# A two-stage attention and mixture-of-experts kernel with another written order

## The chip, the cores and the metric

The kernel runs on one core of a Trainium2 chip, in one launch. The metric is the device time of an execution in microseconds (us), the median of several runs; lower is better. A core has a matrix engine (TensorE, PE in the profile; its weight loads are shown apart as PEld), three engines that work on the elements of tiles (VectorE = DVE, ScalarE = ACT, GpSimd = POOL), and SyncE (SP), which here does nothing but issue DMAs. The engines run side by side, and each takes its own instructions strictly in the order in which the program lists them. They wait for each other by semaphores.

## The reference

The inputs q, k and v hold 8 batches, 8 heads, 576 positions and 64 numbers a head. The first stage is sparse attention: heads 0 to 3 see the last 32 positions ("local"), heads 4 to 7 see every 32nd position back ("strided"). Its result is x, 576 x 512 for each batch. The second stage is a mixture of four experts, each of which is a causal attention with one head of 64; each position uses the two experts with the largest gate logits.

```
scores = where(masks, q @ k.T / 8, -1e9)        # masks: local for heads 0-3, strided for 4-7
x = softmax(scores) @ v                          # heads side by side: 576 x 512 a batch
logits = x @ w_gate                              # 4 experts, the best two kept, softmax over them
for e in range(4):
    a = softmax(causal((x @ wq[e]) @ (x @ wk[e]).T / 8))
    out += weight[e] * (a @ (x @ wv[e]) @ wo[e]) # weight 0 where e is not one of the two
```

## The kernel before

The first stage handles two heads at a time, a "head pair" (hp 0 and 1 local, 2 and 3 strided), in `stage1`: SP loads q, k and v; q and k are transposed, for the first two batches by PE into PSUM banks with copies out of them (`tp`, `tp_out`, lines 570 to 599 and 335), later by DVE (`tq`, line 522); then the scores on PE (`sl`, `s`, lines 627 and 641), the mask and a softmax in six steps that goes between DVE, GpSimd and ACT (lines 655 to 679), a transpose of the weights (`ptl`, or `pt` and `pt_out`) and the product with v (`xal`, `xa`, lines 735 and 754). x is then split into a rounded high part (`xh`, ACT, line 717) and the rest (`xl`, DVE, line 719), so that three fast matmuls stand for one of full precision.

The second stage handles two experts at a time (ep 0 and 1): the projections of q and k (`pj`, lines 907 and 918; for the first two experts of batch 0, line 918, cut into one operation for each head pair, so that they can begin before x is complete), the values and gate logits (`vp`, line 854; for the last rows of two batches together, line 817), scores (`s2`, `s2_4`, lines 992 and 972), mask and maximum on DVE (line 999), exp on ACT (line 1004), scaling by the softmax sum and the gate on GpSimd (`scale2`, lines 1023 and 1029), a transpose on PE (`t2`, line 1048) with copies out of PSUM (`t2_out`, line 335), the product with the values (`acc`, line 1081), and the output projection (`yp`, line 1110) with its copy (`yp_out`, line 335) and store.

None of this is issued in the order in which it is written. The calls only make a list `OPS` of 2573 operations, each of which knows its engine or the two engines that may do it, its dependencies and its buffers. `schedule()` then walks the list ORDER of operation numbers and emits each. So ORDER fixes the order of each engine's queue (what stands earlier in ORDER goes first on its engine), and also which buffer of a ring an operation gets, since a buffer is taken when its first user is emitted. Operations on different engines still run side by side. SECOND is the set of operations that go to the second of their two engines: a copy out of PSUM (`t2_out`, `tp_out`, `pt_out`, `vp_out`, `yp_out`; helper `either`) goes to ACT, and to DVE if it is in SECOND. FILL gives a number of matmuls of an identity matrix with itself that are emitted just before an operation ("filling matmuls", line 298), into a free PSUM bank, if there is one; their result is not used, and they keep PE busy. Before all of them stand five "warm" matmuls (line 1130).

There are 8 PSUM banks; the rings of SBUF buffers for natural q and k hold three (`nat`; pairs 0 and 1 of batch 0 use a tile of the second stage, `p`). Numbers that are needed below: 1 and 2 load q and k of pair 0 of batch 0, 44 and 45 of pair 1, 87 and 88 of pair 2, 122 and 123 of pair 3; 16 and 17 load v of pair 0; 157 to 178 load weights of q and k; 13, 8 and 3 are the transposes of pair 0; 18 its scores, 33 its product with v; 1129 to 1150 are the cut projections of batch 0, 1168 and 1171 the first of its uncut ones, which read x of all four pairs.

Of the kernel before, what the change touches and what calls it, by code (L numbers as in the profile page):

```python
# [20 lines left out]
def attention_moe_kernel(  # L21
# [61 lines left out]
    class Ring:  # L83
# [36 lines left out]
    }  # L120
    ORDER = [
# [1072 lines left out]
```

## Time and profile before

| what | value |
|---|---|
| median of 3 runs (lowest, highest) | 453.73 us (452.95, 453.95) |
| span of the profiled execution, first to last instruction | 452.2 us; its own time beyond the span is not recorded, the median is 1.5 us longer |
| PE busy | 439.5 us, 97% |
| DVE busy | 356.5 us, 79% |
| ACT busy | 264.9 us, 59% |
| GpSimd busy | 221.5 us, 49% |
| granted TensorE clock, mean | 0.995 |
| HBM read and written | 31.20 MB and 9.44 MB |

The profile is one execution. "Busy" is the time in which an engine has at least one instruction under way, and matmuls overlap in a pipeline: a projection's matmul is shown as 0.29 us long, but the next one starts 0.13 us later. What an operation costs PE is therefore read from its start to the start of the next one. [...] A matmul of full precision, such as a filling one, is shown as two instructions.

### The profile page before, as it was taken

The page shows a single profiled execution, that of the slowest core. Times are in us where ns is not written, and L with a number is a line of the kernel's source. Part 1 is how long each engine was busy: PE and PEld are TensorE (multiplying, and loading weights), DVE is VectorE, ACT ScalarE, POOL GpSimd, SP SyncE. Part 2 cuts the span into 40 slices and gives each one's busy share as a digit, 9 for nine tenths or more (in the row PEclk, how much of TensorE's full clock was granted, in tenths as well). Part 3 has the DMA queues.
Part 4 walks back from the last instruction along what each step waited for, and adds up shares of the span by engine and source line. Part 5 has one row for each costly group of instructions (what it writes and reads, how often), then busy time and mean ns, then how long its engine had stood idle before and what let it go on. Part 6 is the DMA issues. An engine that isn't in the chain of part 4 may idle for free.

```text
span 452.2 us, 19227 instructions
## 1 busy us (share of the span) xinstructions
PE 439.5 (97%) x7792; PEld 392.4 (87%) x7792; DVE 356.5 (79%) x1121; ACT 264.9 (59%) x835; POOL 221.5 (49%) x404
## 2 busy tenths in 40 slices
PE   6998999999999999999999999999999999999996
PEld 5887898897899998998899998988988998998875
DVE  4668889989999787769999778789998877466852
ACT  1447647765748455466666566376585477554751
POOL 4163843794563825165647454237743736326330
PEclk9899999999999999999999999999999999999999
DMA  5775465635744524552624525506733201010013
GB/s 146 156 185 159 106 125 120 102 79 83 141 84 89 127 53 101 95 124 57 126 68 93 116 58 117 99 16 127 125 98 89 94 30 53 1 25 25 25 71 116
DMA packets 156272, 41.89 MB, mean 93 GB/s; under 512 B 145976, under 2 KB 149432, under 8 KB 156184
## 3 DMA queue, kind: packets, MB, share of 16 engines
q1 hardware_dynamic: 156184, 40.67, 41.2%
q8 instruction: 61, 1.00, 0.9%
q14 instruction: 27, 0.22, 0.2%
HBM read 31.20 MB, written 9.44 MB: 90 GB/s over the span
## 4 chain that ended last, share of the span: by engine, by line
PE 83%; DVE 9%; ACT 2%; DMA 2%; issue 1%; POOL 1%; SPq 0%; DVEq 0%; ACTq 0%; POOLq 0%
PE bank L907 20%; PE bank L1081 10%; PE bank L854 9%; PE bank L1110 9%; PE bank L992 7%; PE bank L1048 6%; PE bank L735 3%; PE bank L972 3%; PE bank L627 3%; PE bank L754 3%; PE bank L298 3%; PE bank L641 2%; DVE qkt L522 2%; PE bank L705 2%; DVE p L999 1%
## 5 line engine op out<-in xcount | busy, mean ns | idle before, releaser
L1029 POOL TENSOR_SCALAR p<-p,st,wt 128x128 f32<-128x128 f32 (+3 forms) x128 | 77.0, 614 | 51.0 <-DVE st L1013 34.7
L1004 ACT ACTIVATE p<-p,st 128x256 f32<-128x256 f32 (+3 forms) x128 | 71.2, 560 | 8.2 <-DVE st L999 8.2
L999 DVE CUSTOM_DVE_ANT_0 p<-bank,m_cau 128x384 f32<-128x384 f32 (+3 forms) x128 | 57.5, 485 | 4.8 <-PE bank L992 4.1
L1081 PE MATMUL bank<-th,vs 128*64 128x192 f32 (+4 forms) x512 | 48.3, 337 | 0.2 <-DVE th L335 0.2
L522 DVE STREAM_TRANSPOSE qkt<-nat 128x576 f32<-128x576 f32 x48 | 47.4, 1006 | 0.0
L927 ACT CAST qk<-bank 128x288 fp32r<-128x288 f32 x64 | 25.0, 402 | 37.7 <-PE bank L907 34.9
L1081 PEld LDWEIGHTS bank<-th,vs 128*64 128x64 f32 x512 | 34.0, 137 | 13.2 <-issue 6.6
L335 ACT COPY th<-bank 128x256 f32<-128x256 f32 (+2 forms) x105 | 41.3, 433 | 7.1 <-PE bank L1048 6.0
L717 ACT CAST xh<-bank 128x128 fp32r<-128x128 f32 (+4 forms) x112 | 30.0, 321 | 22.6 <-PE bank L754 11.6
L719 DVE TENSOR_TENSOR xl<-bank,xh 128x128 fp32r<-128x128 f32 (+4 forms) x112 | 32.3, 326 | 12.2 <-ACT xh L717 11.8
L1048 PE MATMUL bank<-ident,p 64*128 64x64 f32 x800 | 38.6, 228 | 1.0 <-DVE p1s L655 0.6
L1048 PEld LDWEIGHTS bank<-ident,p 64*128 64x128 f32 x800 | 32.2, 139 | 6.5 <-issue 1.4
L668 POOL TENSOR_TENSOR p1s<-p1s,st 128x648 f32<-128x648 f32 (+1 forms) x18 | 20.8, 1160 | 33.1 <-DVE st L666 30.9
L854 PE MATMUL bank<-wh_v,xh 128*128 128x260 f32 x128 | 36.3, 284 | 0.0
L854 PE MATMUL bank<-wh_v,xl 128*128 128x260 f32 x128 | 36.2, 283 | 0.0
L854 PE MATMUL bank<-wl_v,xh 128*128 128x260 f32 x128 | 36.1, 282 | 0.0
L907 PE MATMUL bank<-xh,wh_q 128*128 128x288 f32 x120 | 36.0, 300 | 0.0
L907 PE MATMUL bank<-xh,wh_k 128*128 128x288 f32 x120 | 35.6, 297 | 0.0
L907 PE MATMUL bank<-xl,wh_q 128*128 128x288 f32 x120 | 35.4, 295 | 0.0
L907 PE MATMUL bank<-xl,wh_k 128*128 128x288 f32 x120 | 35.4, 295 | 0.0
L907 PE MATMUL bank<-xh,wl_q 128*128 128x288 f32 x120 | 35.3, 294 | 0.0
L907 PE MATMUL bank<-xh,wl_k 128*128 128x288 f32 x120 | 35.3, 294 | 0.0
(182 smaller groups left out, 1286.0 us busy)
## 6 DMA issues: line engine op xcount, KB each, us to landing
out_dram<-ys SPq DMA_DIRECT2D x32, 256.0 KB
nat<-in_k_dram SPq DMA_DIRECT2D x96, 72.0 KB
nat<-in_q_dram SPq DMA_DIRECT2D x96, 72.0 KB
v<-in_v_dram SPq DMA_DIRECT2D x96, 40.0 KB
v<-in_v_dram SPq DMA_DIRECT2D x48, 54.0 KB
v<-in_v_dram SPq DMA_DIRECT2D x32, 48.0 KB
v<-in_v_dram SPq DMA_DIRECT2D x32, 45.0 KB
out_dram<-ys SPq DMA_DIRECT2D x8, 128.0 KB
```

What stands on the lines that cost most here:

```text
L335: (nc.scalar.copy if e == "ACT" else nc.vector.tensor_copy)(dst, src)
L522: op("tq", {"DVE": 0.66 if local else 1.11}, k0 - 13, lambda e, x=x: nc.vector.transpose(turned(qkt.t, x), raw(x) if local else raw(x).rea ...
L719: op("xl", {"DVE": dve(n_)}, key + 0.5, lambda e, s_=s_, x_=x_: nc.vector.tensor_sub(x_(xl.t), s_(xa.t), x_(f(xh.t))), r=[xa, xh[u]], w=[x ...
L854: nc.tensor.matmul(vp.t[:, :NV], xx.t[:, t0:t0 + 128], ww.t[:, kt, :], start=i == 0, stop=i == 11)
L907: nc.tensor.matmul(pj.t[:, :HS], ww.t[:, kt, ep * 128:(ep + 1) * 128], xx.t[:, c], start=i == 0, stop=i == 11)
L992: nc.tensor.matmul(sp[a].t[:, :nk], x.t[r, 0, q0:q0 + 128], y.t[r, 1, :nk], start=i == 0, stop=i == 2)
L999: lambda e, sp=sp, p=p, a=a, nk=nk, ci=ci: nc.vector.tensor_tensor_reduce(out=p.t[:, a, :nk], in0=sp[a].t[:, :nk], in1=m_cau[:, S - nk:], ...
L1004: op("exp2", {"ACT": 0.285 + 0.00084 * nk}, k_ + 1, lambda e, p=p, a=a, ci=ci, nk=nk: nc.scalar.activation(p.t[:, a, :nk], p.t[:, a, :nk], ...
L1029: lambda e, p=p, a=a, ci=ci, t=t, nk=nk: nc.gpsimd.tensor_scalar(p.t[:, a, :nk], p.t[:, a, :nk], st.t[:, 20 + ci + a:21 + ci + a], wt.t[:, ...
L1048: nc.tensor.transpose(tp[hf].t[:, 64 * c:64 * c + 64], src, ident[r, r])
L1081: nc.tensor.matmul(acc.t[o, c0:c0 + cn], vw, th[a].t[:, s0:s0 + cn], start=j == 0, stop=j == idx[-1], skip_group_check=True)
L1110: nc.tensor.matmul(yp.t[:, :DM], xx.t[:, c0:c0 + 128], ww.t[:, ep, :], start=i == 0, stop=i == 5)
```

## The change

The three tables are replaced; the operations, their code, their buffers and the rings stay the same. By engine the lists say:

| operations that may go to two engines | before | after |
|---|---|---|
| `t2_out` | 105 ACT, 55 DVE | 119 ACT, 41 DVE |
| `tp_out` | 35 ACT, 21 DVE | 40 ACT, 16 DVE |
| `pt_out` | 23 ACT, 9 DVE | 27 ACT, 5 DVE |
| `yp_out` | 21 ACT, 15 DVE | 23 ACT, 13 DVE |
| `vp_out` | 20 ACT, 12 DVE | 17 ACT, 15 DVE |
| `xf` | 38 ACT, 26 GpSimd | 32 ACT, 32 GpSimd |
| `tq_out` | 4 ACT, 8 GpSimd | 6 ACT, 6 GpSimd |
| filling matmuls in FILL | 77 at 33 places | 26 at 11 places |
| of them with a free bank | 67 | 22 |

The cut diff shows the head of ORDER and FILL whole. The rest of ORDER is permuted in the same way.

```diff
     ORDER = [
-        87, 2, 1, 0, 13, 8, 16, 10, 3, 11, 14, 15, 45, 9, 12, 7, 4, 6, 5, 18, 19, 21, 44, 46, 49, 88, 23, 20, 47, 22,
-        172, 173, 166, 48, 59, 123, 25, 51, 17, 52, 56, 58, 169, 122, 201, 181, 54, 55, 57, 92, 53, 27, 50, 61, 24, 26,
-        28, 29, 31, 93, 60, 89, 91, 30, 62, 64, 90, 66, 94, 63, 96, 32, 65, 68, 33, 67, 127, 70, 69, 97, 71, 98, 99, 72,
-        129, 202, 128, 124, 100, 239, 36, 38, 40, 73, 41, 170, 74, 126, 75, 39, 125, 102, 76, 83, 77, 37, 78, 157, 213,
-        104, 101, 240, 84, 215, 208, 203, 106, 34, 103, 35, 160, 171, 209, 214, 131, 158, 205, 183, 105, 159, 204, 107,
-        174, 1135, 132, 212, 206, 161, 207, 175, 79, 210, 241, 133, 278, 134, 211, 81, 135, 246, 137, 277, 182, 250,
...
+        2, 0, 1, 13, 44, 8, 12, 45, 15, 14, 3, 10, 56, 6, 46, 87, 7, 11, 57, 88, 9, 5, 4, 51, 58, 53, 55, 18,
+        48, 20, 22, 50, 89, 47, 19, 16, 52, 54, 24, 49, 122, 123, 21, 17, 90, 92, 26, 28, 23, 25, 91, 94, 27,
+        202, 29, 31, 93, 201, 59, 239, 61, 63, 62, 64, 96, 30, 124, 65, 32, 66, 68, 127, 97, 126, 67, 128, 99,
+        98, 101, 100, 125, 240, 33, 129, 169, 131, 70, 69, 203, 60, 102, 38, 71, 104, 40, 72, 172, 36, 103, 207,
+        132, 133, 105, 157, 208, 74, 134, 34, 204, 37, 213, 39, 35, 278, 210, 41, 214, 209, 205, 206, 215, 212,
+        277, 73, 75, 135, 170, 308, 241, 244, 246, 247, 76, 106, 250, 173, 81, 211, 79, 80, 136, 251, 83, 77,
+        85, 171, 307, 248, 95, 245, 160, 158, 78, 218, 138, 107, 163, 174, 137, 84, 1147, 242, 82, 130, 219,
...
     ]
     FILL = {
-        13: 6, 3: 3, 18: 5, 51: 4, 92: 8, 89: 1, 96: 1, 33: 4, 127: 1, 124: 7, 76: 3, 1135: 6, 218: 1, 1136: 1, 282: 1,
-        110: 1, 1148: 2, 316: 1, 1131: 4, 1143: 4, 295: 1, 1388: 1, 1206: 1, 1298: 1, 1237: 1, 1408: 1, 1564: 1, 1473:
-        1, 1712: 1, 2070: 1, 2242: 1, 2547: 1, 2550: 1,
+        0: 4, 3: 1, 8: 3, 13: 1, 18: 3, 56: 1, 96: 1, 124: 2, 241: 4, 246: 2, 1137: 4,
     }
```

## Rows read from the trace of the kernel before

**Rows 1.** The page, busy time of each engine (us, share of the span, instructions):
```profile
PE 439.5 (97%) x7792; PEld 392.4 (87%) x7792; DVE 356.5 (79%) x1121; ACT 264.9 (59%) x835; POOL 221.5 (49%) x404
```

**Rows 2.** The page, shares of the chain that ended last, by engine:
```profile
PE 83%; DVE 9%; ACT 2%; DMA 2%; issue 1%; POOL 1%; SPq 0%; DVEq 0%; ACTq 0%; POOLq 0%
```

**Rows 3.** Busy time by stretch (us), then clock, DMA share and GB/s:
```profile
10.30:56.30 46.00, 43.19 (x1067) 38.55 (x1068) 34.05 (x87) 26.31 (x74) 21.27 (x28) 0.96 0.63 153
60.00:150.00 90.00, 88.53 (x1874) 78.89 (x1873) 82.24 (x250) 60.59 (x191) 49.16 (x85) 1.00 0.56 106
100.00:140.00 40.00, 39.98 (x915) 33.40 (x919) 38.04 (x116) 24.85 (x74) 19.81 (x33) 1.00 0.53 97
150.00:453.00 303.00, 297.27 (x4805) 265.61 (x4803) 232.13 (x736) 175.07 (x565) 144.32 (x268) 1.00 0.34 78
```

**Rows 4.** The same for the filling matmuls of line 298 alone:
```profile
10.30:56.30 46.00, 15.32 (x96) 13.16 (x96) 0.96 0.63 153
60.00:453.00 393.00, 6.24 (x26) 3.89 (x26) 1.00 0.39 84
```

**Rows 5.** PE's timeline near the end: start, length, line, operation:
```profile
437.47 0.46 PE L1048 MATMUL bank<-ident,p 64*128 64x64 f32 x8
437.86 0.49 PE L298 MATMUL bank<-ident 128*128 128x128 f32 x2
438.28 0.46 PE L1048 MATMUL bank<-ident,p 64*128 64x64 f32 x8
```

**Rows 6.** GpSimd's timeline there, the scaling ahead of those transposes:
```profile
435.67 1.52 POOL L1029 TENSOR_SCALAR p<-p,st,wt 128x512 f32<-128x512 f32 x2 [4.00 <-DVE st L1013]
```

**Rows 7.** SP's timeline, the first DMAs that it issues:
```profile
2.79 1.11 SPq L502 DMA_DIRECT2D nat<-in_q_dram  x3
3.94 0.36 SPq L497 DMA_DIRECT2D p<-in_k_dram  x1
4.34 0.43 SPq L497 DMA_DIRECT2D p<-in_q_dram  x1
```

**Rows 8.** PE's timeline after the first load; idle time before and its end in brackets:
```profile
10.24 0.44 PE L583 MATMUL bank<-ident,p 128*128 128x128 f32 x2 [2.27 <-DMA p<-in_q_dram]
...
12.42 1.06 PE L570 MATMUL bank<-ident,p 128*128 128x128 f32 x4
13.28 1.71 PE L298 MATMUL bank<-ident 128*128 128x128 f32 x10
...
16.27 0.66 PE L570 MATMUL bank<-ident,p 128*128 128x128 f32 x4
16.76 0.50 PE L298 MATMUL bank<-ident 128*128 128x128 f32 x3
```

**Rows 9.** Busy time by stretch around the first load, as in rows 3:
```profile
7.90:10.20 2.30, 0.07 (x1) 0.00 (x0) 0.00 (x0) 0.00 (x0) 0.00 (x0) 1.00 1.11 236
10.20:14.20 4.00, 3.96 (x21) 3.96 (x22) 1.44 (x4) 1.66 (x4) 0.00 (x0) 0.57 0.90 179
14.20:20.00 5.80, 5.72 (x121) 5.32 (x120) 3.87 (x10) 2.14 (x6) 1.45 (x2) 1.00 0.59 126
```

**Rows 10.** PE's timeline, the first uncut projection of batch 0:
```profile
56.19 0.29 PE L907 MATMUL bank<-xh,wh_k 128*128 128x288 f32 x1
```

**Rows 11.** Copies out of PSUM: ns shortest/median/longest, first and last start, forms:
```profile
L335 ACT COPY th<-bank x105: 352/427/534, 90.2 to 439.1; 128x384 f32<-128x384 f32 x45, 128x256 f32<-128x256 f32 x41, 128x320 f32<-128x320 f32 x19
L335 DVE COPY th<-bank x55: 377/480/558, 98.6 to 441.8; 128x256 f32<-128x256 f32 x23, 128x384 f32<-128x384 f32 x19, 128x320 f32<-128x320 f32 x13
L335 DVE COPY qkt<-bank x21: 389/428/496, 10.7 to 49.1; 64x256 f32<-64x256 f32 x11, 64x128 f32<-64x128 f32 x6, 128x324 f32<-128x324 f32 x4
L335 DVE COPY ys<-bank x15: 680/691/692, 144.2 to 445.8; 128x512 f32<-128x512 f32 x15
L335 DVE COPY vs<-bank x14: 391/419/431, 148.6 to 399.8; 128x260 f32<-128x260 f32 x12, 64x256 f32<-64x256 f32 x2
L335 DVE COPY pt<-bank x9: 454/485/496, 50.5 to 382.6; 128x324 f32<-128x324 f32 x9
```

274 rows, old and new, of tables (ORDER, SECOND) are left out of this document.

## The prediction

> **What bounds the kernel now.** I read the page's busy line first, then the chain of waits, then busy time by stretch, then TensorE's own instructions. The busy line puts PE at 97% and DVE at 79% [rows 1]; the chain, which follows the end back to what released it, is PE for 83% and DVE for 9% [rows 2]. The stretches say where this holds. From 60 us on PE is busy 88.53 of 90 us, then 297.27 of 303 us, of which the last 4 are the drain of the output [rows 3]: it idles for about 2.6 us in all. From 10 to 56 us, while batches 0 and 1 are loaded and their first attention is computed, nothing is full: PE 43.19 of 46 us, DVE 34.05, ACT 26.31 [rows 3]. A busy PE is not all work there. The filling matmuls (line 298) take 15.32 us of PE time in 10.3 to 56.3 us and 6.24 us after 60 [rows 4]. So there are two places to gain: the start, and whatever stands on PE's queue after 60 us without computing anything. DVE is the second limit: in 100 to 140 us it is busy 38.04 of 40 us beside a PE with 39.98 [rows 3].
>
> **The change, part by part.** PE's real work is the same 461 operations. I sum against the profiled span of 452.2 us; the median of the runs shown is 453.73, so 1.5 us lie around the span.
>
> *Filling matmuls after 60 us.* The trace has 26 filling instructions there [rows 4]; a filling matmul is two, so 13. The new FILL table has none so late: its last keys, 246 and 1137, stand at positions 130 and 248 of the list. One costs 0.42 us: it starts at 437.86 and the transpose behind it at 438.28 [rows 5]. Does it cover a wait? The transpose at 438.28 reads what GpSimd scaled in the pair of instructions from 435.67, done at 437.19 [rows 6], before the filler began, so here nothing is covered. If all 13 are like that, the change saves 13 x 0.42 = 5.5 us; if each only sits in a wait, nothing. I take 4.5 us: PE hardly waits in this part, but some of the fillers stand around 100 us, where DVE has no room, and there part of it will come back as a wait for DVE.
>
> *The first loads.* SP issued the q half of head pair 2 (three DMAs, 1.11 us) ahead of k and q of pair 0 [rows 7], and PE sat idle 2.27 us for the latter [rows 8]. The new list issues pair 0 first (2, 1), then pair 1 (44, 45), then pair 2 (87, 88). At least the 1.11 us of issue go; the 295 KB ahead in the queues are 1.25 us more at the 236 GB/s moved just then [rows 9]. Bounds: 0, if something else holds the first transpose, and 2.27, the whole idle time. I take 1.5, nearest to the issue row. What moves back in exchange are v of pair 0 (16, 17) and the weights (169, 172, 157 ...), behind x of several pairs. Their first readers, values1 of pair 0 (33) and the first projection, also stand later (positions 82 and 160 instead of 74 and 133), so I charge nothing. Were that wrong, PE would wait in the start with projections queued behind.
>
> *The start, 10 to 56 us.* The landmark is the first projection that needs all four head pairs of batch 0 (1168 or 1171); it began at 56.19 us [rows 10]. Ahead of it the old lists put 81 DVE and 77 ACT operations, the new ones 74 and 72, with the same 49 on PE. Five of DVE's seven are copies of transposed q and k (0.43 us each [rows 11]). The fillers ahead of it also go from 54 issued to 22, by my count of free banks, so transposes and scores stand less behind fillers. Seven operations at 34.05 us / 87 instructions, 0.39 us, are 2.7 us of DVE time; at its 74% share of that stretch 3.7 us. Upper bound of the gain: 5 us, if the fillers on PE had also been delaying the producers. [...] I take 1.5 us, under half.
>
> *DVE to ACT.* Of the copies that may run on either, the lists move 14 t2_out, 5 tp_out, 4 pt_out and 2 yp_out to ACT and 3 vp_out back. On DVE that frees 14 x 0.480 + 5 x 0.428 + 4 x 0.485 + 2 x 0.691 - 3 x 0.419 = 10.9 us [rows 11] and puts somewhat less on ACT (a t2_out copy is 0.427 us there [rows 11]), which is busy 59% [rows 1] and hides it. By itself this shortens nothing, as PE ends the chain; it is what lets PE take the 4.5 us without meeting DVE. If it isn't enough, the second rival holds.
>
> *New waits.* A new order can bring waits that no trace of before shows. PE's idle time after 60 us is 2.6 us; I bound the new one by none and by double, -2.6 to +2.6 us, and charge 0.5. Behind a waiting transpose (t2) stand projections and value matmuls that are ready, on PE's one queue, and the copies on ACT and DVE wait for them.
>
> Sum: -4.5 - 1.5 - 1.5 + 0.5 = -7.0 us; the span becomes 445.2, and with 1.5 around it 446.7 us.
>
> [...]
>
> **The rivals.** *One: as forecast*, 446.7 us, own range 443.5 to 449.5.
>
> *Two: DVE takes the gain.* PE's 4.5 us turn into waits for DVE, and what the start gains is asked back, since DVE's postponed work meets a full DVE. For it: 38.04 of 40 us in 100 to 140 [rows 3]. Against it: the 10.9 us moved to ACT, and 232 of 303 us after 150, where there is room. A third of the fillers' gain stays and 1 us of the start: 453.7 - 2.5 = 451.2 us.
>
> [...]
>
> *Four: the start gains all it can* (5 us, 2.27 us of load, 5.5 us of fillers, no new waits): 453.7 - 12.8 = 440.9 us. For it: DVE's and the load's bounds are from rows; against: all have to come at once while DVE is full.
>
> *Five: nothing,* the fillers were standing in waits that remain: 453.7 us. Rows 5 and 6 speak against it.
>
> **How the numbers follow.** Chances: one 0.51, two 0.24, three 0.10, four 0.10, five 0.05. About 0.2%, 0.9 us, is what a measurement of this kernel can tell from no change. Faster by more (under 452.8): one, two and four, 0.85; same: five, 0.05; slower: three, 0.10. The range leaves out three, five and half of four: 442.0 to 452.8 us.
>
> **What would show it.** Fillers: line 298 gone after 60 us, and PE idle there still under about 4 us. Loads: the first transpose of pair 0 (line 583) starts at 8 to 9 us. Start: the first projection of the second pair of experts (line 907) before 54 us. DVE: th copies near 119 on ACT and 41 on DVE, DVE busy under 350 us. [...] The forecast is wrong if PE's idle time after 60 us grows by more than the 5.5 us of fillers, or if line 907 begins later than 56.2 us.

## The result, and the profile after

The changed kernel takes 448.51 us (median of 4 runs, 447.87 to 448.86) against 453.34 us for the kernel before beside it: 0.9901 of its time, 95% interval 0.9877 to 0.9925, or 4.8 us less. The forecast was 446.7 us with an own range of 443.5 to 449.5. The profiled execution took 448.27 us, its span is 446.6. Code lines have numbers higher by 7 than before (298 is now 305, 907 is 914).

The changed kernel's page, busy time by engine and the chain of waits [rows 1, 2]:

```profile
PE 429.5 (96%) x7702; PEld 384.2 (86%) x7702; DVE 344.8 (77%) x1099; ACT 270.7 (61%) x853; POOL 221.0 (49%) x408
PE 74%; DVE 5%; issue 2%; ACT 1%; DMA 1%; SPq 0%; POOL 0%; DVEq 0%
```

PE is busy 10 us less and still ends the chain. Its busy time by stretch in the changed kernel [rows 3]:

```profile
10.30:56.30 46.00, 40.25 (x1021) 36.34 (x1020) 35.79 (x88) 28.07 (x81) 21.15 (x28) 0.85 0.64 150
60.00:150.00 90.00, 86.68 (x1782) 77.79 (x1781) 78.89 (x238) 57.12 (x185) 52.57 (x91) 1.00 0.56 109
150.00:446.00 296.00, 289.99 (x4754) 258.64 (x4752) 222.08 (x719) 180.45 (x577) 139.25 (x261) 1.00 0.34 78
```

Two things stand out: between 60 and 150 us PE now idles 3.3 us (it was 1.5), and the granted clock of the start, a share of full speed, is 0.85. Where the gain lies is read from the landmark of the prediction, the first uncut projection [rows 10]; in the changed kernel's timeline of PE:

```profile
50.41 0.29 PE L914 MATMUL bank<-xh,wh_k 128*128 128x288 f32 x1
```

It begins 5.78 us earlier. The stretch from there to the end of PE's last matmul, first of the kernel before, then of the changed one:

```profile
56.19:448.40 392.21, 389.58 (x6706) 348.31 (x6704) 318.15 (x992) 236.81 (x760) 195.71 (x354) 1.00 0.39 84
```

```profile
50.41:442.80 392.39, 386.26 (x6683) 345.69 (x6681) 309.14 (x977) 243.63 (x779) 199.66 (x363) 1.00 0.39 85
```

392.2 and 392.4 us: the whole gain lies ahead of the landmark. Behind it the fillers' time (13 fillers, 5.2 us in the trace of before, from the start of each to the start of what follows) is gone from PE's queue, PE's idle time grew from 2.6 to 6.1 us, and nothing is saved.

**What stands in its place.** The longest waits of PE in the changed kernel, by line and what ended them (total, times, longest):

```profile
PE bank L634 <- issue: 4.7, 3, 2.1
PE bank L634 <- DVE qkt L342: 1.5, 2, 1.0
PE bank L305 <- POOL ident masks.py:199: 1.4, 1, 1.4
PE bank L742 <- DVE pt L702: 1.0, 1, 1.0
PE bank L761 <- DVE st L1006: 0.9, 1, 0.9
PE bank L634 <- DVE xl L726: 0.8, 2, 0.6
PE bank L999 <- DVE xl L726: 0.7, 1, 0.7
PE bank L648 <- issue: 0.7, 1, 0.7
```

"issue" is a pause in which the engine waited for nothing that the profile shows. In the kernel before one such wait stood, in the same code line:

```profile
PE bank L627 <- issue: 1.1, 1, 1.1
```

One of the new pauses, in PE's timeline of the changed kernel: score 745 and, right behind it, score 778, 160 small matmuls together, cut after 150 of them:

```profile
214.89 1.76 PE L634 MATMUL bank<-qkt 64*32 64x64 f32 x150
218.29 0.32 PE L634 MATMUL bank<-qkt 64*32 64x64 f32 x10 [1.63 <-issue]
```

The page of the changed kernel has a DMA queue for instructions (packets, MB, share of the DMA engines):

```profile
q8 instruction: 61, 1.00, 0.9%
```

61 packets for 1.00 MB is 16 KB each; with the 15612 records that TensorE left in the trace (matmuls, weight loads and its sequencer's own) that is one packet for every 256 instructions, so the packets are taken here as TensorE's own. Numbering these records from 0 in order of their start, the pauses marked "issue" end at the following ones. A step is the time from the start of one record to the start of the next. The row of 74.68 us is the wait that the view puts down to DVE (L761, `st`); that DVE instruction had ended at 74.30 us, and the pause falls on the same place as the others, so it is counted with them.

```
kernel    instruction          ends at us   step us   after the packet landed, us
before     3265 = 193 + 12x256     82.88      1.34     1.41
changed     449 = 193 +  1x256     18.06      2.32     1.75
changed    3009 = 193 + 11x256     74.68      1.12     1.40
changed    5569 = 193 + 21x256    135.53      1.21     1.42
changed    8385 = 193 + 32x256    218.29      1.85     1.44
changed    9153 = 193 + 35x256    235.98      0.88     1.52
```

Every one falls on the same place in a group of 256. The reading: a group's packet is asked for about when the group ahead of it begins (in the five rows of the changed kernel its transfer starts 0.5 to 2.1 us behind that group's first instruction and lands 0.9 to 1.3 us later), so a group that PE gets through in less than some 3 us ends in a wait for the next. The groups that end in these pauses behind 60 us lasted 2.9 to 3.3 us, of which 1.4 to 2.1 without the pause: they lie almost wholly in the small matmuls of `sl`, `s` and `xa`. Not every short group pays: the one that begins at 336.23 us in the changed kernel took 2.21 us without a pause, and the one at 342.50 us in the kernel before 2.74; there the next packet's transfer had begun 0.8 to 1.1 us ahead of the group.

Behind the landmark the sum is then: fillers -5.2, pauses 5.06 - 1.34 = +3.7, total +0.2 us; what is left over, +1.7, is a remainder and was not read from any row. This sum says where PE's time went, not what would come back without the pauses; that is tested below.

**The start.** SP's first transfers in the changed kernel [rows 7], and PE's first transpose of pair 0 [rows 8]:

```profile
0.80 0.40 SPq L504 DMA_DIRECT2D p<-in_k_dram  x1
1.25 0.90 SPq L504 DMA_DIRECT2D p<-in_q_dram  x2
```

```profile
7.38 0.38 PE L590 MATMUL bank<-ident,p 128*128 128x128 f32 x2
```

SP issues its first load at 0.80 instead of 2.79 us, and the transpose comes 2.86 us earlier. But the granted clock (the number ahead of the last two) falls to 0.50 twice in the changed kernel [rows 9]:

```profile
17.00:27.20 10.20, 9.14 (x233) 8.14 (x233) 7.51 (x19) 4.34 (x13) 5.63 (x8) 0.50 0.67 175
34.00:37.50 3.50, 3.30 (x86) 3.13 (x87) 3.10 (x11) 3.38 (x10) 3.44 (x6) 0.51 0.56 147
```

The first fall, at 16.98 us, lies inside the pause for instructions that ends at 18.06 us. If that pause brought the clock down, it cost more than its 2.3 us; runs below test this. The second fall, at 34.04 us, came among three steps of 0.8 to 1.3 us that the view gives as waits for DVE.

### The profile page after: what moved, and what is told of

Read it like the earlier page. It is cut to its first block, busy times and chain, and to the rows that moved or that the text cites. A ratio compares the mean times of both kernels' runs of the same rounds, so it can differ in the third digit from the quotient of the medians.

```text
span 446.6 us, 19071 instructions
## 1 busy us (share of the span) xinstructions
PE 429.5 (96%) x7702; PEld 384.2 (86%) x7702; DVE 344.8 (77%) x1099; ACT 270.7 (61%) x853; POOL 221.0 (49%) x408
## 4 chain that ended last, share of the span: by engine, by line
PE 74%; DVE 5%; issue 2%; ACT 1%; DMA 1%; SPq 0%; POOL 0%; DVEq 0%
PE bank L914 20%; PE bank L1117 11%; PE bank L861 9%; PE bank L1088 9%; PE bank L999 6%; PE bank L1055 5%; PE bank L979 3%; PE bank L742 3%; PE bank L761 2%; PE bank L634 2%; PE bank L648 2%; DVE qkt L529 1%; PE bank L712 1%; PE bank L824 1%; DVE p L1006 1%
## 5 line engine op out<-in xcount | busy, mean ns | idle before, releaser
L1036 POOL TENSOR_SCALAR p<-p,st,wt 128x512 f32<-128x512 f32 (+3 forms) x128 | 76.6, 610 | 39.7 <-DVE st L1020 17.3
L1011 ACT ACTIVATE p<-p,st 128x512 f32<-128x512 f32 (+3 forms) x128 | 71.7, 568 | 0.4 <-DVE st L1006 0.3
L1006 DVE CUSTOM_DVE_ANT_0 p<-bank,m_cau 128x128 f32<-128x128 f32 (+3 forms) x128 | 57.3, 481 | 6.5 <-PE bank L999 5.0
L342 ACT COPY th<-bank 128x384 f32<-128x384 f32 (+2 forms) x119 | 46.1, 438 | 15.6 <-PE bank L1055 11.8
L724 ACT CAST xh<-bank 128x128 fp32r<-128x128 f32 (+4 forms) x112 | 28.9, 323 | 22.4 <-PE bank L761 11.9
L726 DVE TENSOR_TENSOR xl<-bank,xh 128x128 fp32r<-128x128 f32 (+4 forms) x112 | 32.2, 323 | 13.1 <-ACT xh L724 12.4
L675 POOL TENSOR_TENSOR p1l<-p1l,st 128x640 f32<-128x640 f32 (+1 forms) x18 | 20.5, 1141 | 32.6 <-DVE st L673 31.4
L1055 PE MATMUL bank<-ident,p 64*128 64x64 f32 x800 | 36.0, 226 | 0.4 <-DVE ofl L1101 0.2
L936 DVE TENSOR_TENSOR qkl<-bank,qk 128x288 fp32r<-128x288 f32 x64 | 27.8, 444 | 10.2 <-ACT qk L934 9.9
```

The source lines that it names most:

```text
L342: (nc.scalar.copy if e == "ACT" else nc.vector.tensor_copy)(dst, src)
L724: op("xh", {"ACT": act(n_) + 0.04 * (not local)}, key, lambda e, s_=s_, x_=x_: nc.scalar.copy(x_(xh.t), s_(xa.t)), r=[xa], w=[xh[u]])
L726: op("xl", {"DVE": dve(n_)}, key + 0.5, lambda e, s_=s_, x_=x_: nc.vector.tensor_sub(x_(xl.t), s_(xa.t), x_(f(xh.t))), r=[xa, xh[u]], w=[x ...
L1006: lambda e, sp=sp, p=p, a=a, nk=nk, ci=ci: nc.vector.tensor_tensor_reduce(out=p.t[:, a, :nk], in0=sp[a].t[:, :nk], in1=m_cau[:, S - nk:], ...
L1011: op("exp2", {"ACT": 0.285 + 0.00084 * nk}, k_ + 1, lambda e, p=p, a=a, ci=ci, nk=nk: nc.scalar.activation(p.t[:, a, :nk], p.t[:, a, :nk], ...
L1036: lambda e, p=p, a=a, ci=ci, t=t, nk=nk: nc.gpsimd.tensor_scalar(p.t[:, a, :nk], p.t[:, a, :nk], st.t[:, 20 + ci + a:21 + ci + a], wt.t[:, ...
```

## The experiments

Times are medians beside a median of the kernel before from the same chip; ratios are to it.

### The fillers behind 60 us

```diff
+    FILL = {k: f for k, f in FILL.items() if ORDER.index(k) < 300}
```

> The kernel before without its 13 filling matmuls behind 60 us; orders, engine choices and the start are as before. Theory of the prediction (the fillers stand in nobody's wait, nothing comes back): all 5.3 us that they take on PE go, about 448.0 us. Theory of instruction groups (in both traces PE's long 'issue' pauses end exactly at its instructions number 193 + 256k, about 1.4 us after a 16 KB packet of instructions landed, and no group of 256 took less than 2.9 to 3.25 us): taking out 52 instructions moves the borders of the groups onto stretches of small matmuls; worked out from the trace of before, the pauses behind 30 us grow from 1.3 to 1.9 us to 5.9 us (new ones near 277, 326 and 337 us), so only about 1.3 us is left of the gain: about 452.0 us. Theory of DVE (PE meets a full DVE instead): most of the gain is lost too, but as waits for DVE between 60 and 150 us, not as pauses marked 'issue' near 277 to 337 us.

Measured: 451.41 us (before 453.56), ratio 0.9957, interval 0.9936 to 0.9977: -2.15 us of 5.2. In the trace each removed filler does bring what follows some 0.4 to 0.6 us forward, and then it is lost in lumps. In the kernel before without late fillers, PE at the place of the one pause of the kernel before:

```profile
79.08 1.20 PE L628 MATMUL bank<-qkt 64*32 64x64 f32 x88
81.92 0.97 PE L628 MATMUL bank<-qkt 64*32 64x64 f32 x72 [1.64 <-issue]
```

This step grows from 1.34 to 1.85 us, and new steps of 0.4 to 0.9 us come at 282, 332, 335 and 344 us, also at borders of groups, some 2.6 us in all; waits for GpSimd and DVE grow by 0.7. The groups predicted 4 us or more and places 5 to 7 us earlier: they are a part of it, not all. (That no group took less than 2.9 us, as the expectation says, is not so; the exceptions stand above.) In the profiled runs only 1.0 us lies behind the landmark (391.2 against 392.2 us); the other 1.1 us lie ahead of it, where nothing was changed and the two executions differ all the same, so what the medians gained beyond the 1.0 us isn't placed.

### The same, with the number of instructions kept

```diff
                 for _ in range(o.fill):
+                    if i in LATE:
+                        nc.tensor.matmul(bank[:32, :2], ident[:, :32], ident[:, :2], start=True, stop=True)
+                        continue
                     nc.tensor.matmul(bank[:, :128], ident, ident, start=True, stop=True)
```

> As the run without the 13 late fillers, but each is replaced by a filling matmul of 32 weights and 2 columns, which takes hardly any time and keeps the number of PE's instructions, so every group of 256 begins at the same operation as in the kernel before. Instruction groups: pauses as before (1.3 to 1.9 us), so nearly all of the fillers' time goes, 5.3 us less some 0.06 us for each: about 448.8 us, some 3 us faster than the kernel without any. DVE: the same loss as without fillers, about 452 us. Nothing comes back at all: 448 to 449 us, and the kernel without fillers as fast as this one.

Measured: 451.01 us, ratio 0.9952 (0.9929 to 0.9975). The expectation missed: between large operations such a sliver still costs 0.15 us, so that only 0.27 us of each 0.42 go, about 2.9 us in all, of which 2.55 were kept by the medians. The pause near 81 us is 1.5 us and no new one over 0.5 us comes. In the profiled run 1.3 of the 2.9 us lie behind the landmark. That keeping the borders keeps what is saved isn't shown by this run: it doesn't separate from the one without fillers (451.41).

### Only the number of instructions

```diff
         for _ in range(5):
             nc.tensor.matmul(wb.t[:, :256], ones[:, :128], ones, start=True, stop=True)
+        for _ in range(42):
+            nc.tensor.matmul(wb.t[:32, :2], ones[:, :32], ones[:, :2], start=True, stop=True)
```

> The kernel before with 42 matmuls of 32 weights and 2 columns behind the five warming ones, 168 instructions more for PE while it waits for the first loads; nothing else is changed. Instruction groups: the borders of all groups move 168 instructions back; from the trace of before the pauses behind 30 us grow from 1.9 to 8.3 us, so about 6 us slower, 459 to 460 us, as pauses marked 'issue' that end at instructions 193 + 256k, at other operations than before. Any other theory (waits for DVE, for loads, the clock): no change, 453.3 us, at most 1 us if the extra matmuls delay the first transpose.

Measured: 459.74 us (before 453.56), ratio 1.0143 (1.0111 to 1.0174): +6.2 us, as the groups said and no other theory. The first transpose begins at 10.74 us, 0.5 later; from the landmark to PE's last matmul it takes 398.8 us instead of 392.2. PE's "issue" waits and two of the pauses in this kernel:

```profile
PE bank L627 <- issue: 5.5, 4, 2.3
```

```profile
284.90 1.68 PE L627 MATMUL bank<-qkt 64*32 64x64 f32 x146
287.78 0.34 PE L627 MATMUL bank<-qkt 64*32 64x64 f32 x14 [1.21 <-issue]
```

```profile
334.94 1.77 PE L627 MATMUL bank<-qkt 64*32 64x64 f32 x155
338.96 0.31 PE L627 MATMUL bank<-qkt 64*32 64x64 f32 x5 [2.25 <-issue]
```

They end at instructions 11201 = 193 + 43x256 and 12737 = 193 + 49x256, in operations where the kernel before has no pause at all; the queue has 62 packets instead of 61. A third, of 2.0 us, ends at 84.44 us in place of the 1.34 of before. These steps make 4.5 of the 6.5 us behind the landmark. Another 1.3 us come right behind the last pause: the granted clock fell to 0.50 there and stayed at it until 343.31 us:

```profile
339.89:343.31 3.42, 3.42 (x34) 2.65 (x30) 2.49 (x6) 1.17 (x4) 0.00 (x0) 0.50 0.02 5
```

The kernel before, then, stood at a lucky place: by an estimate from its trace (each group that would take under 3 us is made up to 3) it has 1.5 us of pauses, and shifts of its borders by 1 to 255 give 0.2 to 7.5, half of them over 5.

### The small matmuls kept apart

```diff
+    ORDER.remove(298)
+    ORDER.insert(ORDER.index(1181), 298)
+    ORDER.remove(613)
+    ORDER.insert(ORDER.index(1425) + 1, 613)
+    ORDER.remove(778)
+    ORDER.insert(ORDER.index(1643) + 1, 778)
+    ORDER.remove(811)
+    ORDER.insert(ORDER.index(1769), 811)
```

> The changed kernel with four entries of its order moved, so that no group of 256 instructions of TensorE lies wholly in small matmuls: xa 298 ahead of score 1181, sl 613 behind projection 1425, sl 778 behind projection 1643, s 811 ahead of 1769. Theory of instruction groups: the pauses at 135.5, 218.3 and 236.0 us go and most of that at 74.7, together some 4.5 of 5.1 us; 444 us. Rival: these pauses only stand where PE would wait anyway for DVE's copies and masks (DVE is busy 77%), so they come back as waits for DVE: 448.5 us.

Measured: 447.58 us (before 453.27), ratio 0.9877 (0.9845 to 0.9909). The four pauses are gone from the trace, but the stretch from the landmark to the end only shrinks from 392.4 to 391.4 us. One pause of 0.95 us comes at another border (201.81 us), and waits for ACT and DVE grow by some 1.3 us, as the rival had it; where the rest went wasn't followed. The medians don't separate (447.58 and 448.51, with intervals that overlap). So the pauses are real, but taking them out gave back 1.0 of some 4 us: they are not the whole reason why the changed kernel saves nothing behind the landmark. The other reasons stay open. Where only pauses were added, by the 168 instructions, they were paid in full.

The profiled execution, the fastest of six, gave something else. Up to 65 us its order is the changed kernel's, but its clock stayed at full in the start:

```profile
17.00:27.20 10.20, 8.93 (x259) 7.89 (x258) 9.81 (x28) 6.11 (x19) 6.41 (x9) 1.00 0.72 184
```

Its pause for instructions ended at 17.09 instead of 18.06 us, and its first uncut projection began at 46.95 instead of 50.41 us. Of the 3.46 us, 0.45 are an earlier first transpose and 0.5 a shorter pause; the other 2.5 us go with the clock: operation by operation, the lead grows from 1.0 us at 18.06 to 3.4 us at 27.09 us of the changed kernel, while that is at half clock. This is one pair of executions.

### The clock of the start

```diff
+    FILL[61] = 4
```

> The changed kernel with four filling matmuls (1.7 us, 16 instructions) ahead of sl 61, where PE pauses 2.3 us for instructions (15.7 to 18.06 us) and where the granted clock fell to 0.50 until 27.2 us; the model of the groups gives the same pauses behind 30 us. Theory (this pause is what brings the clock down, and the half clock costs what the first 50 us differ between two runs of the same order, 3.5 us): clock 1.0 from 17 to 27 us, first uncut projection near 47 instead of 50.4 us, 445 us. Rival (the clock falls for the small matmuls and transposes that follow, whatever stood ahead): clock 0.5 there again, 448.5 us, or somewhat more for the fillers.

Measured: 446.49 us (before 454.17), ratio 0.9834 (0.9799 to 0.9870), so some 2 to 3 us better than the changed kernel's 0.9901. In the profiled run, the slowest of six, the pause ended at 17.9 us and its step was no shorter (2.7 us), and the clock fell 0.8 us behind it, for 3.4 us instead of 10.2 (0.83 on average from 17 to 27.2 us), and again at 32.4 us; the projection began at 49.30, 1.1 us earlier. Of this 0.8 us are an earlier first transpose (6.56 us), which the edit can't have moved. The median moved the theory's way, but the trace doesn't show by what; the clock wasn't kept, only its first fall shortened.

```diff
+    FILL.update({13: 6, 3: 3, 18: 5, 51: 4, 92: 8, 89: 1, 33: 4, 124: 7, 76: 3, 1135: 6})
```

> The changed kernel with 10 more entries of filling matmuls in its start (counts as in the kernel before). In the changed kernel the granted clock was 0.50 from 17 to 27 us and 0.51 from 34 to 37.5 us. Theory (the half clock delays the start): with the fillers the clock is 1.0 there and the first uncut projection begins 1 to 2 us earlier than 50.4 us; 447 us. Rival (in the start DVE, ACT and the loads set the pace, and the fillers stand in the way): the clock is 1.0 and the projection begins no earlier; 448.5 to 450 us. About 130 more instructions also move the borders of the groups, by the model for 0.5 to 1 us more pauses.

Measured: 452.84 us (before 453.27), ratio 0.9994 (0.9974 to 1.0014). The clock was 1.00 from 8 to 42 us, and the projection began at 51.89 instead of 50.41: so many fillers cost more than the clock gives back. The further instructions (160 by the trace, not 130) also brought other pauses (237, 281, 330 and 344 us, 5.5 us together). The rival was right on the start; its time, 448.5 to 450 us, was missed by about what these pauses take.

```diff
+    FILL[61] = 4
+    ORDER.remove(298)
+    ORDER.insert(ORDER.index(1181), 298)
...
```

> Both edits on the changed kernel: the four moved entries that keep small matmuls apart at the borders of instruction groups (alone 447.6 us), and the four filling matmuls ahead of sl 61. If the clock of the start is what makes that kernel's runs spread from 443.8 us (clock 1.000) to 449.2 (0.99): 444 us, with the spread gone. Rival: 447.6 us as without them.

Measured: 446.33 us (before 454.17), ratio 0.9848 (0.9811 to 0.9884). The spread did not go: 444.6 to 449.0 us, with mean clocks of 0.987 to 1.000. This kernel has the same four moves. No pause for instructions is left ahead of 20 us, yet in the profiled run the clock still fell, at 31.4 us, behind a step of PE of 1.5 us that ended at 28.9 and one of 0.8, and inside a second one of 0.8 us. The theory that the one pause sets the clock is too narrow: here it fell among waits for DVE. The four moves again shorten the stretch behind the landmark by 1.0 us (393.5 to 392.5), and the medians of the two kernels with the fillers don't differ (446.49 and 446.33).

### The first loads

```diff
+    ORDER.remove(87)
+    ORDER.insert(ORDER.index(1) + 1, 87)
```

> The kernel before with one entry of the order moved: the load of head pair 2 (87) behind the two loads of pair 0 instead of ahead of them. Theory: pair 0's loads were queued on SP behind a load that waits for DVE's clearing of its buffer, so the first transpose comes near 7.5 to 8 us instead of 10.24, and the first uncut projection 1.5 to 2.5 us earlier than 56.2; about 451.3 us. Rival (in the start DVE and ACT set the pace, and the load of pair 2 is then missed): the first transpose comes earlier but the projection does not, 453 us.

Measured, on the kernel before: 450.27 us (before 453.56), ratio 0.9923 (0.9907 to 0.9939), -3.3 us: more than expected. SP's queue in this run:

```profile
0.80 0.39 SPq L499 DMA_DIRECT2D p<-in_k_dram  x1
1.25 0.42 SPq L499 DMA_DIRECT2D p<-in_q_dram  x1
2.79 1.03 SPq L504 DMA_DIRECT2D nat<-in_q_dram  x3
```

and DVE's clearing of the buffers `nat` there:

```profile
2.58 0.70 DVE L322 MEMSET nat<- 128x64 f32 x9
```

The load of pair 2 goes at 2.79 us in either kernel, here with SP free from 1.67 us on, since it writes a buffer that DVE clears first; pair 0's loads had only been standing behind it on SP. The first transpose came at 6.75 us and the projection at 51.57, 3.5 and 4.6 us earlier. PE no longer sat idle ahead of the first transpose, and its clock was 1.00 from 10.2 to 14.2 us, where the kernel before had 0.57 [rows 9]; most of the 1.1 us gained behind the transpose fits that.

```diff
+    ORDER.remove(87)
+    ORDER.insert(ORDER.index(2), 87)
```

> The changed kernel with one part undone: the load of head pair 2 (87) is first in the order again, ahead of the loads of pair 0, as in the kernel before; everything else is the new order. Moved alone in the kernel before, this load was worth 3.3 us. If the parts add up, the changed kernel loses 3.3 us here: 451.8 us, and the rest of the change is worth only some 1.5 us. Rival (the new order of the start, with fewer fillers and fewer copies ahead of the projections, is what made it insensitive): the first transpose comes 2 to 3 us later, but the first uncut projection less than 1 us, 449 us.

Measured, on the changed kernel: 451.38 us (before 454.14), ratio 0.9942 (0.9917 to 0.9967). Against the changed kernel's 0.9901 this part is worth 0.4%, 1.9 us, between the two theories. Its profiled run was the slowest of twelve (455.27 us), so nothing is read from its trace here.

### The engine choices alone

```diff
     SECOND = {
-        4, 5, 7, 11, 15, 42, 43, 55, 58, 85, 86, 112, 125, 147, 155, 159, 165, 168, 174, 180, 185, 188, 191,
...
+        4, 6, 12, 14, 15, 47, 50, 52, 53, 54, 58, 86, 128, 146, 147, 162, 165, 168, 171, 174, 177, 180, 185, 191, 197,
...
```

> The changed kernel with the engine choices of the kernel before: 25 of the copies that it moved to ACT go back to DVE, 3 the other way, some 11 us of DVE time. By the prediction the moved copies are what lets PE run without meeting DVE: without them PE waits for DVE more, 1 to 3 us, 450 to 451 us. Rival: DVE has room even so (344.8 + 11 us of 446), and the choice is worth nothing: 448.5 us.

Measured: 463.68 us (before 453.27), ratio 1.0235 (1.0205 to 1.0264). Five times as much as the larger of the expectations. And the other way round, the new choices under the old order:

> The kernel before with the engine choices of the changed kernel: 11 us of DVE time go to ACT, the order stays. The reverse exchange (the new order with the old choices) cost 15 us. Theory one (what counts is DVE's load): DVE is relieved here, so 453.4 us or up to 2 us less. Theory two (each choice fits the place where its operation stands in the order; exchanged in either direction, copies land on an engine that is just then busy, and PE waits behind them): slower here too, by 5 to 15 us, 458 to 468 us, in many waits of 0.3 to 1.5 us, though DVE is busy less.

Measured: 467.12 us (before 454.17), ratio 1.0297 (1.0258 to 1.0336), with DVE busy only 346.8 us. PE's waits, first of the new order with the old choices, then of the old order with the new ones:

```profile
PE bank L635 <- ACT p1l L678: 2.5, 1, 2.5
PE bank L1000 <- DVE st L1007: 1.6, 2, 1.4
PE bank L1118 <- DVE ys L343: 1.5, 1, 1.5
```

```profile
PE bank L640 <- ACT nat L525: 1.5, 1, 1.5
PE bank L1047 <- DVE qkl L928: 1.2, 1, 1.2
PE bank L1080 <- ACT th L334: 0.8, 2, 0.6
```

Waits for ACT and for DVE stand side by side in both, spread over the span. DVE's load is not what counts: 8 us more of it cost 15 us in one order, and 10 us less of it cost 13 us in the other. Pauses at the borders of groups don't explain it either: over 0.3 us they make 5.9 us behind the landmark in the first (5.7 in the changed kernel) and 2.3 in the second (1.3 before). What fits is that ORDER sets where a copy stands in its engine's queue, and SECOND which queue that is; one table without the other puts copies behind work that they were not meant to wait for. Which copy does it at which place was not followed one by one. The exchange also moves `xf` and `tq_out` between ACT and GpSimd, so it is not of DVE and ACT alone.

### A version that beats both

```diff
+    FILL = {k: f for k, f in FILL.items() if ORDER.index(k) < 300}
+    ORDER.remove(87)
+    ORDER.insert(ORDER.index(1) + 1, 87)
...
+        for _ in range(10):
+            nc.tensor.matmul(wb.t[:32, :2], ones[:, :32], ones[:, :2], start=True, stop=True)
```

> The kernel before with three small edits: the load 87 behind those of pair 0 (measured alone: -3.3 us), no filling matmuls behind 60 us (alone -2.1 us, of 5.3 taken out), and 10 tiny matmuls behind the warming ones, which move the borders of the instruction groups 40 on. Theory of instruction groups: with this number no border falls badly (modelled pauses 0.1 us, against 3.5 us of steps seen without fillers and 1.3 in the kernel before), so the fillers' time goes except some 1.7 us of waits: 450.3 - 5.5 + 1.7 - 1.3 = 445.2 us. Rival: only the two single gains add up, 453.4 - 3.3 - 2.1 = 448.0 us.

Measured: 445.81 us (before 453.27), ratio 0.9838 (0.9815 to 0.9861), 7.5 us faster than the kernel before and clear of the changed kernel's interval. No wait marked "issue" is left among PE's waits, and PE's busy time between 60 and 150 us is the highest of all runs:

```profile
60.00:150.00 90.00, 88.79 (x1885) 79.78 (x1884) 82.37 (x252) 58.52 (x186) 52.04 (x89) 1.00 0.59 112
```

From the landmark to PE's last matmul it takes 387.6 us against 392.2. The fillers' 5.2 us and the one pause of before, 1.3, are gone from there; 4.6 of these 6.5 us are really saved, against none in the changed kernel. The rival's sum, 448.0 us, lies outside the interval (444.9 to 447.0 us). A run with the two single edits and without the 10 tiny matmuls was not made, but the trace without late fillers stands beside this one: its steps of over 0.3 us at borders, 4.0 us behind the landmark, are all gone here, and the stretch is 3.7 us shorter (391.2 to 387.6). In the old order, then, the pauses were what ate the fillers' time.

## Why the prediction was right, and where only its sum was

The total was right to 1.8 us and the sign was; the terms were not what the forecast said, and two errors cancelled: behind the landmark nothing was saved where 4.0 us were forecast, and ahead of it 5.8 us where 3.0 were. That the total came out is luck.

*Filling matmuls after 60 us, -4.5.* Line 305 does not appear behind 60 us, and one filler took 0.42 us, as read from [rows 5]. What failed is the term "new waits, +0.5": behind the landmark all of it came back. PE's time shows 3.7 us more of pauses for instructions and 1.7 us of remainder in its place; but without four of the pauses only 1.0 us was given back, so the pauses are a part of the cause in this order, and the rest is open. The bound put on them, -2.6 to +2.6, was drawn from PE's idle time before; a resource that happened not to bind there (one pause, 1.34 us) gave no bound. Alone, the same removal saves 2.15 us by the medians, and with the borders moved to a good place as well most of it. The condition named for the forecast's failure, PE's idle time growing by more than 5.5 us, was the wrong gauge: it grew by 3.5 and the term failed all the same, since PE's shown busy time, whose ends are modelled, fell by 3.3 us and not by the fillers' 5.2.

*The first loads, -1.5.* The mechanism was right, the size off: 3.3 us alone, 1.9 in the new order. The upper bound of 2.27 was PE's idle time ahead of the first transpose in one execution, and no bound: that idle time was 3.24 us in the run without late fillers, whose start has the same order, and 1.1 us more came behind the transpose. The step that the forecast missed is that pair 2's load waits on SP for a memset by DVE, with pair 0's queued behind it.

*The start, -1.5.* With the loads it gave 5.8 instead of 3.0 us, although the clock took some back. How the 2.5 to 3.9 us that the loads leave divide among fewer copies, fewer fillers and the new order was not run.

*DVE to ACT, "shortens nothing by itself".* Wrong: alone it lengthens the kernel by 13 us, and without it the new order loses 15. The working treated the 28 choices as a sum of durations moved from a fuller engine to an emptier one. They are part of the order.

*Rival two* (DVE takes the gain) had the right shape, a gain eaten behind 60 us, but DVE's waits are the lesser part in the changed kernel's view; without the four pauses they grow. *Rival three* (0.10 on a slower kernel, by the clock in the start) showed in the granted clock, which was 0.50 for 10.2 us from 16.98 and for 3.4 us from 34.04, but not in the time. PE was busy for 12.4 us of them; four transposes took 0.86 us at 0.50 and 0.49 at 1.00 [rows 8], and at that price, an estimate, this costs 12.4 x 0.37 / 0.86 = 5.3 us. The undisturbed start of the same order puts it at 2.5: part of the start waits for other engines anyway. The fall at 16.98 us came in a gap of PE, and that at 339.89 us of the kernel with 168 more instructions 0.9 us behind one. Those gaps were pauses for instructions, and not a lack of fillers against loads. Not every gap does it: in the same order, in the run with the small matmuls kept apart, the clock stayed at 1.00 through one of 1.8 us.

## What to carry to other kernels

Where an engine runs many small instructions, count them: in these traces the steps that end at numbers 193 + 256k were waits for code (0.88 to 2.32 us in the table above), 168 instructions put ahead moved them to other operations and cost 6.2 us, and so a change in order should be judged at several shifts before its small gains are believed. A pause that is taken away is not a gain yet: in the old order it was, in the new one only a quarter of it came back. A gain on the engine that ends the chain is only as large as the next wait allows, and waits that don't bind in the trace of before have no row there to bound them by. An order and an assignment to engines that were made together should be priced together.

## What the runs showed of the hardware

In the traces of all kernels here, 39 steps of over 0.75 us between two of TensorE's instructions fall at numbers 193 + 256k, and every one ends 1.26 to 1.75 us after an instruction packet has landed. 168 instructions of hardly any work, placed where PE waited for loads, cost 6.2 us later on. A matmul of 32 weights and 2 columns costs 0.06 us in a row of its kind in the start and 0.15 us between large ones. The granted clock fell to 0.50 inside a 2.3 us pause in the changed kernel, and 0.9 us behind one of 2.5 us in the kernel with the 168 instructions, and stayed up through one of 1.8 us in the changed kernel's order; with four fillers ahead of the first pause it was not held, but was at 0.50 for 3.4 instead of 10.2 us there.
